# Three fused matmul stages on one core: operand addresses of the wide products, landing times in the planner, and the pace of the second MLP's weight conversions

## Chip, core and metric

One core of a Trainium2 chip runs the whole program. The metric is the device time of one execution in microseconds; the median of three runs is given. The program uses TensorE (products), VectorE and ScalarE (element-wise work), GpSimd (some transfers) and SyncE's queue (most transfers).

## What is computed

A linear attention without softmax, whose output goes through two MLPs, all to float32 accuracy:

```python
kv = np.einsum('bhsd,bhse->bhde', k, v)            # 8 x 8 heads, 576 tokens, 64 wide
out = np.einsum('bhsd,bhde->bhse', q, kv)
x = out / np.sqrt(np.mean(out * out, -1) + 1e-6) * g_norm   # 4608 tokens x 512

h = x @ w_in                                       # 512 -> 2048
x = (s * np.maximum(h, 0) ** 2 + b) @ w_out        # 2048 -> 512
h = x @ w_in2
return (h * np.cos(h)) @ w_out2
```

The MLP weights arrive as float64, the rest as float32, and the weights are turned into float32 pairs on the chip.

## The kernel before

**Products.** A *product* is one MATMUL instruction: 128x128 weights are loaded (LDWEIGHTS) and 256, 384 or 512 columns stream through them from SBUF into a PSUM bank. To keep float32 accuracy every operand is split into a high and a low part of type float32r, and one mathematical product is three instructions: high x high, high x low, low x high. Each product has its own weight load, and the weights of the next product load while the present one streams.

**Stages.** Up to about 360 us: attention, interleaved with the first three blocks of 512 tokens of the first MLP. There `mm_h` (L724 to L726) streams x (512 columns, tiles X in the tile `shared`) through w_in (tiles WI), `act1` makes g (tiles G), and `mm_o` (L781, for the first twelve weight tiles of block 0 L773 in plain float32) streams g through w_out (tiles WO). From there on the work goes in *pairs* (two tiles of 128 hidden columns, 768 tokens): 32 pairs for the rest of the first MLP (about 362 to 880 us), then 48 for the second. `mm_h2` (L932) computes h by a scheme with seven instead of eight half-size block multiplications: seven *chains* of six products of 384 columns, in the order 0, 1, 5, 4, 6, 2, 3. It streams sums and differences of quarter blocks of x (`x_sums`; slots in `shared`, G, `late` and WI) through prepared weight sums that `w_load` brings in from DRAM into the ring WI[0:6]. ScalarE copies the chains' banks out (`snap`, L944), VectorE adds them to h (L948). In the first MLP `act1_pair` (L1002, L1003, L1005, L1007) makes g as high and low parts in WI[6:], and `mm_o1` (L827) streams them through w_out, 512 and 256 columns. In the second MLP `act2` does it, and `mm_o` (L781) has g's parts (in WI[6:] and `raw`) as weights and streams w_out2 (512 columns).

**Conversions.** During the first MLP's pairs the second MLP's 32 weight tiles are converted (`conv2`, `w_conv`): a load of raw bits into the one tile `raw`, ScalarE L382 (the first to need the load) and L392, VectorE L383 to L400, and for w_in2 sums of two tiles (`w_sums`, L454). `split_store` (L436, L437) splits the result into tiles T, which go to DRAM (L444) and come back later as weights. A T tile is free again when its store has landed; `snap` uses the same five T tiles in the first MLP's pairs.

**What sets the order.** Nothing is ordered by hand. Every step is an `op` with an engine, a cost and a due time; `Plan.run` plays them through a model of the engines and queues: at each step it takes the engine that can start first, and on it the op with the earliest due time among those that can start within 0.1 us. A tile slot is given to the op that starts, if the model says that its last reader (for a store, its landing) is done. The order that comes out is the program's order on each engine, and the engines then wait for each other by semaphores. A transfer of the model lands 0.5 us (`LANDS`) after its modelled time on the DMA engines. `sref` makes a tile in a slot; its argument `shift` is an offset in elements from the slot's start, in the tiles WI and RAW alone.

## Time and profile before

| what | value |
|---|---|
| median of 3 runs | 1625.25 us (1623.31 to 1625.88) |
| the profiled execution | 1624.52 us |
| its span, first to last instruction | 1622.7 us |
| TensorE busy | 1610.5 us, 9952 products recorded |
| VectorE, ScalarE busy | 1101.8 us, 872.0 us |
| pairs of the first MLP, undisturbed | 15.64 us each |
| pairs of the second MLP | 15.52 us each |

A float32 product is recorded as two, so 9952 records stand for 8864 instructions; 3504 of them are float32r products of 512 columns, 768 of 256 and 3360 of 384. A product's record starts when it starts to stream and ends when its last column is through, so records overlap: the time of one product in a row of many is the distance between starts, and its record lasts some 0.16 us longer. Idle time of TensorE is therefore seen shortened by that much.

### The profile page before, as it was taken

To read this page: it belongs to the slowest core of one execution; us is meant where nothing else is said; L and a number is where in the kernel's file an instruction comes from. 1 tells how busy PE (TensorE), PEld (TensorE's weight loads), DVE (VectorE), ACT (ScalarE), POOL (GpSimd) and SP (SyncE) were. 2 spreads that over 40 slices of the span, in tenths; PEclk is the share of its full clock that TensorE was granted. 3 is DMA by queue.
4 is the path that set the end of the run, shared out by engine and by line. 5 is a ranking of instruction groups with operands and counts; after the bars stand their busy time and mean duration, and the time that the engine had idled before them with its cause. 6 is when DMAs were issued, how large, how long until landed. Compare 5 with 4: busy or idle time off the path is not lost.

```text
span 1622.7 us, 26185 instructions
## 1 busy us (share of the span) xinstructions
PE 1610.5 (99%) x9952; PEld 1423.7 (88%) x9952; DVE 1101.8 (68%) x1832; ACT 872.0 (54%) x1483; POOL 54.5 (3%) x90
## 2 busy tenths in 40 slices
PE   8999999999999999999999999999999999999998
PEld 7668888789999999989999989989899898998997
DVE  6887776675776777776446667667668668568564
ACT  5865543355565565555435455545546546446543
POOL 0011222100000000000000000000000000000000
PEclk9999999999999999999999999999999999999999
DMA  9746878936778878876656445544444544444531
GB/s 319 224 102 175 217 192 204 249 123 227 246 232 267 274 218 276 261 224 203 223 180 229 160 123 149 169 124 139 167 131 136 172 117 137 164 133 129 156 117 47
DMA packets 198285, 297.44 MB, mean 183 GB/s; under 512 B 81936, under 2 KB 124432, under 8 KB 198160
## 3 DMA queue, kind: packets, MB, share of 16 engines
q1 hardware_dynamic: 191568, 274.20, 54.5%
q0 software_dynamic: 6016, 20.45, 4.6%
q8 instruction: 79, 1.29, 0.3%
q10 hardware_dynamic: 576, 1.11, 0.2%
q14 instruction: 46, 0.38, 0.1%
HBM read 232.79 MB, written 62.91 MB: 182 GB/s over the span
## 4 chain that ended last, share of the span: by engine, by line
PE 94%; DMA 3%; DVE 1%; ACT 1%; issue 0%; POOL 0%; SPq 0%; ACTq 0%; POOLq 0%; DVEq 0%
PE banks L932 35%; PE banks L781 30%; PE banks L827 14%; PE banks L724 3%; PE banks L773 3%; PE banks L725 3%; PE banks L726 3%; PE banks L550 1%; PE banks L644 1%; DMA raw<-in_moe_w_out_dram 1%; PE banks L682 1%; DMA w2i_d<-t 1%; DMA wi<-w1i_d 1%; PE banks L1019 1%; DMA raw<-in_moe_w_in_dram 0%; DMA x_d<-t 0%
## 5 line engine op out<-in xcount | busy, mean ns | idle before, releaser
L932 PE MATMUL banks<-shared,wi 128*128 128x384 f32 x2232 | 441.0, 336 | 0.8 <-ACT t L944 0.7
L932 PEld LDWEIGHTS banks<-shared,wi 128*128 128x128 f32 x2232 | 390.6, 188 | 13.8 <-ACT t L944 2.2
L781 PE MATMUL banks<-wo,wi 128*128 128x512 f32 x1446 | 372.6, 391 | 0.0
L781 PEld LDWEIGHTS banks<-wo,wi 128*128 128x128 f32 x1446 | 269.9, 188 | 49.9
L827 PE MATMUL banks<-wi,wo 128*128 128x512 f32 (+1 forms) x1536 | 288.6, 336 | 0.8 <-DVE wi L1007 0.8
L827 PEld LDWEIGHTS banks<-wi,wo 128*128 128x128 f32 x1536 | 244.1, 188 | 29.7 <-DVE wi L1007 1.3
L944 ACT COPY t<-banks 128x384 f32<-128x384 f32 x235 | 112.3, 479 | 215.2 <-PE banks L932 199.1
L986 ACT ACTIVATE wi<-wi 128x768 f32<-128x768 f32 x96 | 81.3, 847 | 79.6 <-DVE wi L984 79.6
L932 PE MATMUL banks<-late,wi 128*128 128x384 f32 x552 | 111.7, 336 | 0.0
L932 PE MATMUL banks<-g,wi 128*128 128x384 f32 x504 | 110.1, 337 | 1.0 <-ACT t L944 0.8
L781 PE MATMUL banks<-g,wo 128*128 128x512 f32 x432 | 108.3, 394 | 0.0
L978 ACT ACTIVATE wi<-wi 128x768 f32<-128x768 f32 x95 | 79.9, 846 | 46.2 <-DVE wi L948 44.9
L932 PEld LDWEIGHTS banks<-late,wi 128*128 128x128 f32 x552 | 97.2, 188 | 3.3
L948 DVE TENSOR_TENSOR wi<-banks,t 128x384 f32<-128x384 f32 x128 | 71.2, 556 | 40.3 <-PE banks L932 33.9
L781 PEld LDWEIGHTS banks<-g,wo 128*128 128x128 f32 x432 | 79.9, 188 | 17.3
L932 PEld LDWEIGHTS banks<-g,wi 128*128 128x128 f32 x504 | 89.2, 188 | 6.5 <-ACT t L944 2.2
L982 DVE SCALAR_TENSOR_TENSOR wi<-wi,wi 128x768 f32<-128x768 f32 x95 | 90.8, 956 | 1.7
L988 DVE TENSOR_TENSOR wi<-wi,wi 128x768 f32<-128x768 f32 x95 | 90.6, 954 | 1.5
L781 PE MATMUL banks<-wo,raw 128*128 128x512 f32 x282 | 88.3, 393 | 0.0
L980 DVE TENSOR_SCALAR wi<-wi 128x768 f32<-128x768 f32 x96 | 53.7, 559 | 50.2 <-ACT wi L978 48.9
L724 PE MATMUL banks<-shared,wi 128*128 128x512 f32 x192 | 82.4, 429 | 2.5 <-ACT shared L701 1.6
L1003 DVE SCALAR_TENSOR_TENSOR wi<-wi,small,wi 128x768 f32<-128x768 f32 x64 | 64.8, 1016 | 23.5 <-ACT wi L1002 23.3
(155 smaller groups left out, 2090.9 us busy)
## 6 DMA issues: line engine op xcount, KB each, us to landing
wi<-w2i_d SPq DMA_DIRECT2D x144, 512.0 KB, 4.2
wi<-w1i_d SPq DMA_DIRECT2D x96, 512.0 KB, 4.7
late<-x_d SPq DMA_DIRECT2D x36, 384.0 KB, 6.0
w2i_d<-t SPq DMA_DIRECT2D x48, 256.0 KB, 4.5
wi<-w2i_d SPq DMA_DIRECT2D x48, 256.0 KB, 2.7
x_d<-t SPq DMA_DIRECT2D x40, 256.0 KB, 3.0
wi<-in_moe_w_in_dram SPq DMA_DIRECT2D x16, 512.0 KB, 9.2
wo<-in_moe_w_out_dram SPq DMA_DIRECT2D x16, 512.0 KB, 9.6
```

What stands on the lines that cost most here:

```text
L724: nc.tensor.matmul(h.t, wh, hi, start=(c == 0), stop=False)
L781: nc.tensor.matmul(o.t, a, b, start=(first and z == 0), stop=(last and z == 2))
L827: nc.tensor.matmul(dst, x[:, sl], y[:, src], start=(first and z == i == 0), stop=(last and z == 2), skip_group_check=a >= 4)
L932: nc.tensor.matmul(o.t[:, 0:HT], a, b, start=(first and c == z == 0), stop=(c == 1 and z == 2), skip_group_check=not first)
L944: op("ACT", 0.38, by + 1, lambda: nc.scalar.copy(dst(), o.t[:, 0:HT]), p=[s], r=[o])
L948: op("DVE", 0.475, by + 1, lambda: nc.vector.tensor_tensor(out=h[f].t[:, half * HT:(half + 1) * HT], in0=a.t[:, 0:HT], in1=s.t, op=ALU.add ...
L978: op("ACT", act, by, lambda u=u, x=x: nc.scalar.activation(u.t, x.t, AF.Identity, scale=1.0 / TWO_PI, bias=0.25), w=[u], r=[x])
L980: op("DVE", two, by + 1, lambda u=u: nc.vector.tensor_scalar(out=u.t, in0=u.t, scalar1=MAGIC, scalar2=-MAGIC, op0=ALU.add, op1=ALU.add), w ...
L982: op("DVE", one, by + 2, lambda u=u, x=x: nc.vector.scalar_tensor_tensor(out=u.t, in0=x.t, scalar=1.0 / TWO_PI, in1=u.t, op0=ALU.mult, op1 ...
L986: op("ACT", act, by + 4, lambda u=u: nc.scalar.activation(u.t, u.t, AF.Sin, scale=TWO_PI, bias=0.5 * math.pi), w=[u])
L988: op("DVE", one, by + 5, lambda u=u, x=x: nc.vector.tensor_tensor(out=u.t, in0=u.t, in1=x.t, op=ALU.mult), w=[u], r=[x])
L1003: op("DVE", 0.93, by + 2, lambda u=u, x=x: nc.vector.scalar_tensor_tensor(out=u.t, in0=u.t, scalar=s_sb, in1=x.t, op0=ALU.mult, op1=ALU.mu ...
```

## The change

Three edits go together.

**Addresses.** `sref` takes a table from a slot's prefix to an offset, and the tiles that it shifts begin elsewhere. Modulo 128 bytes (all tile distances of a kind are multiples of it, so it is the same for a whole line) the difference between the address from which a product streams and the address of the weights of the next product of its line is, in the two built programs:

| products | streamed, weights | before | after |
|---|---|---|---|
| L724 to L726, 512 columns, 576 | X in `shared`, WI | 64 | 16 |
| L781 in the first MLP, 512 columns, 432 | G, WO | 0 | 16 |
| L827, 512 and 256 columns, 768 each | WI, WO | 64 | 16 |
| L781 in the second MLP, 512 columns, 1728 | WO, WI or RAW | 64 | 16 |
| L932, 384 columns, 3360 | `shared`, G, late or WI, ring WI | 64 | 64 |
| L932 followed by L781 of the second MLP | | 64 | 16 |
| L932 followed by L827 | | 0 | 0 |

The streamed tiles move in the first three rows, the weights in the fourth.

**Landing.** An op has a new field `late`, which the planner adds to the landing of a transfer: 2.0 us for the raw loads of the second MLP's weights, 1.5 us for the stores of split weights.

**Pace.** The 32 conversions of the second MLP are called for over 25 pairs instead of 22.

```diff
-    def op(self, eng, cost, due, fn, w=(), p=(), r=(), keep=(), after=()):
+    def op(self, eng, cost, due, fn, w=(), p=(), r=(), keep=(), after=(), late=0.0):
...
-                end = seen = dma + self.LANDS
+                end = seen = dma + self.LANDS + o.late
...
-    shared = sb.tile([P, 33 * 256], F32R, name="shared")
+    EDGE = (4, 16)
+    shared = sb.tile([P, 33 * 256 + EDGE[1]], F32R, name="shared")
+    WIDE = 1024 + 64
...
-                t, at = shared, plan.parts[s].start * 256
-            elif shift and s in WI + RAW:
-                t, at = sb.tile([P, 1024], dtype, tag=s, name=s), shift
+                t, at = shared, plan.parts[s].start // 2 * 256 + EDGE[plan.parts[s].start % 2]
+            elif shift and s[:2] in shift or s in G:
+                t, at = sb.tile([P, WIDE if s in G else 1024], dtype, tag=s, name=s), shift.get(s[:2], 0)
...
+    OFF = {s: 4 for s in slots("g", 3)}
...
-        plan.parts[s] = range(4 * n, 4 * n + 4)
+        plan.parts[s] = range(8 * n, 8 * n + 8)
...
-        plan.parts[s] = range(3 * n, 3 * n + 3)
+        plan.parts[s] = range(6 * n + 1, 6 * n + 7)
...
-        op("SP", 1.45 if kind == "i" else 1.35, by - 12 if load_by is None else load_by, load, w=[raw], after=after)
+        op("SP", 1.45 if kind == "i" else 1.35, by - 12 if load_by is None else load_by, load, w=[raw], after=after,
+           late=2.0 if ph else 0.0)
...
-            op("SP", n * 0.0013, by, store, p=[ref], r=[part])
+            op("SP", n * 0.0013, by, store, p=[ref], r=[part], late=1.5)
...
-            g = sref(G)
+            g = sref(G, shift=OFF)
...
-            x = x2f[j, k, c] = sref(XF if j else XF0, F32R, (2, HT), 16)
+            x = x2f[j, k, c] = sref(XF if j else XF0, F32R, (2, HT), {"wi": 16})
...
-            u, hi, lo = sref(ACTS, F32, (TB2,)), *(sref(PARTS, F32R, (TB2,)) for z in range(2))
+            u, hi, lo = sref(ACTS, F32, (TB2,)), *(sref(PARTS, F32R, (TB2,), {"wi": 12, "ra": 12}) for z in range(2))
...
-            u, hi, lo = sref(ACTS1, F32, (TB2,), 32), *(sref(ACTS1, F32R, (TB2,), 32) for z in range(2))
+            u, hi, lo = sref(ACTS1, F32, (TB2,), {"wi": 20}), *(sref(ACTS1, F32R, (TB2,), {"wi": 20}) for z in range(2))
...
-                done_convs - EARLY_CONVS) * (NP1 - 10) <= (n - 1) * (4 * NU - EARLY_CONVS):
+                done_convs - EARLY_CONVS) * (NP1 - 7) <= (n - 1) * (4 * NU - EARLY_CONVS):
```

The second and third edit change the order on all engines from about 150 us on; up to there it is the same. Lines of the new kernel are five higher from `mm_h` and `act1` on (L944 is L949, L1003 is L1008). Two places follow, with the tiles' numbers.

ScalarE in pair 22, a raw weight's first step (L382, now L387) among the copies of chains (L944, now L949). Before:

```order
L944 COPY t2_7814<-banks_77 128x384
L382 ACTIVATE c2_7816<-raw_7751 128x512
L944 COPY t0_7824<-banks_77 128x384
L944 COPY t4_7841<-banks_77 128x384
L392 ACTIVATE raw_7751<-raw_7751 128x512
```

Now:

```order
L949 COPY t3_7751<-banks_77 128x384
L387 ACTIVATE c3_7785<-raw_7733 128x512
L949 COPY t1_7793<-banks_77 128x384
L949 COPY t2_7799<-banks_77 128x384
L397 ACTIVATE raw_7733<-raw_7733 128x512
```

The raw step still stands between the copies; over the whole program it stands directly ahead of a copy in 18 of 32 conversions before and in 17 of 32 now.

ScalarE from the end of pair 22 to the first copy of pair 23 (the last row of each), where the next block's x is split (L885, now L890). Before:

```order
L1002 ACTIVATE wi14_7864<-wi13_7846 128x768
L436 CAST t0_7871<-c2_7816 128x512
L944 COPY wi8_7804<-banks_77 128x384
L1002 ACTIVATE wi11_7881<-wi8_7804 128x768
L1005 ACTIVATE wi9_7892<-wi14_7864,small_125 128x768
L1005 ACTIVATE wi13_7903<-wi11_7881,small_125 128x768
L382 ACTIVATE c4_7911<-raw_7866 128x512
L885 CAST shared_76<-late3_7407 128x384
L885 CAST shared_76<-t1_7471 128x384
L885 CAST shared_76<-t3_7489 128x384
L392 ACTIVATE raw_7866<-raw_7866 128x512
L944 COPY t2_7957<-banks_77 128x384
```

Now:

```order
L1007 ACTIVATE wi7_7828<-wi6_7808 128x768
L441 CAST t1_7840<-c3_7785 128x256
L1007 ACTIVATE wi15_7844<-wi14_7727 128x768
L441 CAST t3_7858<-c1_7842 128x512
L890 CAST shared_76<-late3_7341 128x384
L890 CAST shared_76<-t4_7470 128x384
L890 CAST shared_76<-t0_7501 128x384
L890 CAST late4_7887<-late0_7324 128x384
L1010 ACTIVATE wi9_7890<-wi7_7828,small_125 128x768
L1010 ACTIVATE wi12_7902<-wi15_7844,small_125 128x768
L441 CAST t2_7906<-c0_7833 128x512
L949 COPY t3_7910<-banks_77 128x384
```

The two steps that make g's high parts (L1005, now L1010) came before the splits and now come after four of them, followed by a split of w_sums' result (L441).

VectorE at the same place. Before:

```order
L948 TENSOR_TENSOR wi13_7846<-banks_77,t2_7814 128x384
L400 ISA c2_7816<-raw_7751,c2_7816 128x1024
L1003 SCALAR_TENSOR_TENSOR wi14_7864<-wi14_7864,small_125,wi13_7846 128x768
L437 TENSOR_TENSOR t4_7883<-c2_7816,t0_7871 128x512
L1003 SCALAR_TENSOR_TENSOR wi11_7881<-wi11_7881,small_125,wi8_7804 128x768
L1007 SCALAR_TENSOR_TENSOR wi10_7901<-wi14_7864,small_125,wi9_7892 128x768
L1007 SCALAR_TENSOR_TENSOR wi8_7913<-wi11_7881,small_125,wi13_7903 128x768
```

Now:

```order
L459 TENSOR_TENSOR c0_7833<-c3_7785,c4_7557 128x256
L459 TENSOR_TENSOR c1_7842<-c3_7785,c0_7833 128x256
L442 TENSOR_TENSOR t2_7846<-c3_7785,t1_7840 128x256
L459 TENSOR_TENSOR c1_7842<-c4_7557,c1_7842 128x256
L459 TENSOR_TENSOR c0_7833<-c3_7785 128x256
L1008 SCALAR_TENSOR_TENSOR wi7_7828<-wi7_7828,small_125,wi6_7808 128x768
L891 TENSOR_TENSOR shared_76<-late3_7341,shared_76 128x384
L891 TENSOR_TENSOR shared_76<-t4_7470,shared_76 128x384
L891 TENSOR_TENSOR shared_76<-t0_7501,shared_76 128x384
L895 TENSOR_TENSOR t4_7470<-t4_7470,late0_7324 128x384
L895 TENSOR_TENSOR t0_7501<-t0_7501,late2_7334 128x384
L1008 SCALAR_TENSOR_TENSOR wi15_7844<-wi15_7844,small_125,wi14_7727 128x768
```

Both L1003 of the pair stood near the raw step L400; now four w_sums (L459), and x's splits and differences (L891, L895) stand ahead of the first or the second L1008.

## Rows read from the trace of the kernel before

**Rows 1.** The page: busy time, share of the span and instructions of each engine.

```profile
PE 1610.5 (99%) x9952; PEld 1423.7 (88%) x9952; DVE 1101.8 (68%) x1832; ACT 872.0 (54%) x1483; POOL 54.5 (3%) x90
```

**Rows 2.** Stretches: start:end, length, busy us by engine, granted clock, DMA share, GB/s.

```profile
378.00:484.00 106.00, 105.22 (x597) 97.04 (x597) 75.09 (x126) 61.88 (x106) 0.00 (x0) 1.00 0.74 243
484.00:738.00 254.00, 252.20 (x1443) 233.81 (x1442) 184.66 (x310) 148.99 (x256) 0.00 (x0) 1.00 0.78 251
738.00:863.00 125.00, 125.00 (x722) 116.92 (x721) 62.69 (x89) 57.99 (x95) 0.00 (x0) 1.00 0.61 206
888.00:1602.00 714.00, 714.00 (x3591) 645.97 (x3590) 485.60 (x724) 375.69 (x592) 0.00 (x0) 1.00 0.45 140
```

**Rows 3.** L781's products, 329 to 332 and 1120 to 1126 us: duration ns min/median/max.

```profile
L781 PE MATMUL banks<-g,wo x12: 388/389/389, 329.2 to 331.7; 128*128 128x512 f32 x12
...
L781 PE MATMUL banks<-wo,wi x23: 388/392/394, 1120.8 to 1125.9; 128*128 128x512 f32 x23
```

**Rows 4.** Timeline of TensorE, three places: start, us, engine, line, what, count.

```profile
327.15 0.39 PE L724 MATMUL banks<-shared,wi 128*128 128x512 f32 x1
...
329.22 2.88 PE L781 MATMUL banks<-g,wo 128*128 128x512 f32 x12
331.94 0.39 PE L724 MATMUL banks<-shared,wi 128*128 128x512 f32 x1
...
342.72 2.92 PE L781 MATMUL banks<-g,wo 128*128 128x512 f32 x12
...
786.85 0.87 PE L827 MATMUL banks<-wi,wo 128*128 128x256 f32 x6
787.55 2.25 PE L932 MATMUL banks<-shared,wi 128*128 128x384 f32 x12
...
794.18 6.38 PE L827 MATMUL banks<-wi,wo 128*128 128x512 f32 x30
800.41 0.85 PE L932 MATMUL banks<-shared,wi 128*128 128x384 f32 x4
...
1119.79 1.20 PE L932 MATMUL banks<-shared,wi 128*128 128x384 f32 x6
1120.83 6.34 PE L781 MATMUL banks<-wo,wi 128*128 128x512 f32 x27
```

**Rows 5.** L932's products, 780 to 830 and 1000 to 1100 us, as rows 3.

```profile
L932 PE MATMUL banks<-shared,wi x81: 332/336/340, 784.8 to 825.3; 128*128 128x384 f32 x81
...
L932 PE MATMUL banks<-shared,wi x204: 336/336/336, 1003.9 to 1097.9; 128*128 128x384 f32 x102
```

**Rows 6.** Timeline near 510 us; in brackets the idle time and its releaser.

```profile
509.44 0.67 ACT L382 ACTIVATE c<-raw 128x512 f32<-128x512 f32 x1 [4.05 <-DMA raw<-in_moe_w_out_dram]
...
510.70 0.97 PE L932 MATMUL banks<-shared,wi 128*128 128x384 f32 x4 [0.66 <-ACT t L944]
```

**Rows 7.** Groups, 380 to 870 us: busy us, mean ns | idle; one timeline row.

```profile
L1003 DVE SCALAR_TENSOR_TENSOR wi<-wi,small,wi 128x768 f32<-128x768 f32 x62 | 62.8, 1017 | 23.5 <-ACT wi L1002 23.3
...
L944 ACT COPY t<-banks 128x384 f32<-128x384 f32 x123 | 58.7, 478 | 95.1 <-PE banks L932 79.1 <-DMA w2i_d<-t 9.2 <-DVE wi L948 1.8
L1005 ACT ACTIVATE wi<-wi,small 128x768 fp32r<-128x768 f32 x62 | 57.6, 933 | 10.9 <-DVE wi L1003 7.7 <-PE banks L827 2.9
...
L948 DVE TENSOR_TENSOR wi<-banks,t 128x384 f32<-128x384 f32 x61 | 33.9, 555 | 28.3 <-PE banks L932 22.0 <-ACT t L944 3.7 <-PE banks L827 1.9
...
L436 ACT CAST t<-c 128x512 fp32r<-128x512 f32 x40 | 24.3, 617 | 7.5 <-DVE c L400 3.9 <-DMA w2i_d<-t 2.5 <-DVE wi L948 0.6
...
L400 DVE CUSTOM_DVE_ANT_0 c<-raw,c 128x1024 uint16<-128x1024 uint16 x32 | 22.0, 688 | 7.1 <-ACT raw L392 6.5
...
L382 ACT ACTIVATE c<-raw 128x512 f32<-128x512 f32 x31 | 20.7, 667 | 39.3 <-DMA raw<-in_moe_w_out_dram 26.8 <-DMA raw<-in_moe_w_in_dram 12.4
...
L454 DVE TENSOR_TENSOR c<-c,c 128x256 f32<-128x256 f32 x24 | 10.1, 420 | 0.3
...
724.10 1.02 DVE L886 TENSOR_TENSOR shared<-t,shared 128x384 fp32r<-128x384 f32 x2
```

More of the change, by code (lines that the diff above doesn't have):

```diff
@@ L83, in __init__ @@
         self.parts = {}
-    def op(self, eng, cost, due, fn, w=(), p=(), r=(), keep=(), after=()):
+    def op(self, eng, cost, due, fn, w=(), p=(), r=(), keep=(), after=(), late=0.0):
         o = Op()
-        o.eng, o.cost, o.due, o.fn, o.refs = eng, cost, due, fn, list(dict.fromkeys([*w, *p, *r, *keep]))
+        o.eng, o.cost, o.due, o.fn, o.late = eng, cost, due, fn, late
+        o.refs = list(dict.fromkeys([*w, *p, *r, *keep]))
         deps = set(after)
@@ L254, in pool_of, with sref @@
         return sb
-    shared = sb.tile([P, 33 * 256], F32R, name="shared")
-    def sref(slots, dtype=F32, shape=(512,), shift=0):
+    EDGE = (4, 16)
+    shared = sb.tile([P, 33 * 256 + EDGE[1]], F32R, name="shared")
+    WIDE = 1024 + 64
+    def sref(slots, dtype=F32, shape=(512,), shift=None):
         def make(s):
@@ L300, in fused_kernel @@
     for s in [*WO, *G, *T, *C]:
-        sb.tile([P, 512 if s in T + C else 1024], F32, tag=s, name=s)
+        sb.tile([P, 512 if s in T + C else WIDE if s in G else 1024], F32, tag=s, name=s)
     sb.tile([P, 48], F32, tag="between", name="between")
@@ L322, in fused_kernel @@
         kv_f[divmod(n, KC)] = sref([KV_F[n]], F32, (D,))
-    small = cpool.tile([P, 20], F32, name="small")
+    small = cpool.tile([P, 8], F32, name="small")
     g_sb, s_sb, b_sb, spare = (small[:, i:i + 1] for i in range(4))
@@ L747, in act1 @@
         if i in WHOLE:
-            g = sref(G)
+            g = sref(G, shift=OFF)
             if i in ON_ACT:
@@ L755, in act1 @@
             return g
-        g = sref(G, F32R, (2, TB))
+        g = sref(G, F32R, (2, TB), OFF)
         op("ACT", 0.62, by - 1, lambda: nc.scalar.activation(g.t[:, 0], t.t, AF.Identity, bias=b_sb),
@@ L920, in mm_h2 @@
         t0 = pair_due(n)
-        h = [sref(ACTS, F32, (TB2,)) if n >= NP1 else sref(ACTS1, F32, (TB2,), 32) for f in range(2)]
+        h = [sref(ACTS, F32, (TB2,)) if n >= NP1 else sref(ACTS1, F32, (TB2,), {"wi": 20}) for f in range(2)]
         order = (0, 1, 5, 4, 6, 2, 3)
```

## The prediction

> **What bounds the kernel now.** I read the page first. TensorE is busy 99% of the span, VectorE and ScalarE 68% and 54% [rows 1], and TensorE's granted clock is 1.00, its upper level of 2.4 GHz, in every stretch [rows 2]. So the time is the sum of the products (one product is one MATMUL instruction), and there are two ways to shorten it: less time from the start of one product to the start of the next, or less waiting. The view by stretches sizes the second: between 738 and 863 us and from 888 us on, TensorE is busy for the whole stretch; between 378 and 738 us it lacks 0.78 + 1.80 us [rows 2]. A wait shows shortened, since the 0.16 us by which a product's record outlasts its successor's start (389 ns against 227 ns [rows 3, 4]) counts as busy; with some seven waits about 3.7 us are lost there. The rest is the rate.
>
> The rate is read from the timeline. Twelve 512-column products of the first MLP's second matmul run from 329.22 to 331.94 us: 2.72 / 12 = 226.7 ns each. The nine before them (L724 to L726) take (329.22 - 327.15) / 9 = 230.0 ns. In the second MLP 27 of them take (6.34 - 0.39) / 26 = 228.8 ns, and at L827, between 794.18 and 800.41 us, 24 of 512 and 6 of 256 columns take 6.23 us; six of 256 columns take 0.70 us (786.85 to 787.55), which leaves 230.3 ns for one of 512 [rows 4]. At 2.4 GHz 512 columns stream in 213.3 ns, so every product has 13 to 17 ns on top. Three things tell me that part of this hangs on where the operands lie. The extra is steady, not noise: the settled products by g last 388 to 389 ns, those by wo 388 to 394 [rows 3]. Between these groups the residue of (address of the streamed operand minus address of the next weights, modulo 128 bytes) differs: 0 for g, 64 for the other three. And the 384-column products, residue 64 among themselves, last exactly 336 ns in a stretch of the second MLP, but up to 340 where the first MLP's L827, with residue 0, comes next [rows 5].
>
> **The change, part by part.** *Residue 16 for all products of 512 and 256 columns.* No row has residue 16, so the price is bounded from rows. Nearest to 16 is 0, and the settled row of residue 0 is 226.7 ns; that is the value I take. L781 of the second MLP: 1728 x (228.8 - 226.7) = 3.6 us. L827: 768 x (230.3 - 226.7) = 2.8 us. L724 to L726: 576 x (230.0 - 226.7) = 1.9 us. L781 of the first MLP is at 0 now; a run of twelve takes 2.72 us when settled, and the most it could give is 432 x 3.3 ns = 1.4 us; I take 0.5. The 768 products of 256 columns: 0, since no row shows them at another residue; bounds 768 x 4 ns = 3 us either way. Where a 384-column product is followed by L781 (some 185 places) the residue goes from 64 to 16: 0 to 185 x 4 ns = 0.7 us lost [rows 5], I take 0.4. The 384-column products keep 64: nothing. Sum: -8.4 us. Bounds of this term: below, the 256-column products, whose extra is 116.7 - 106.7 = 10.0 ns, would make a 512-column product 223.3 ns, 3504 x (229.2 - 223.3) = -21 us (229.2 is the mean of the four rates above, by count); above, what residue 0 does to a 384-column product, +4 ns, is 3504 x 4 = +14 us. The other end of the shift costs nothing I can find: the shifted tiles are written and read by VectorE and ScalarE alone, no DMA touches them, and both engines have slack [rows 1].
>
> A rule of the Trainium skill speaks against this part. SBUF — State Buffer, section "Who interferes with whom", gives TensorE two independent read ports, one for the streamed operand and one for weights, and has TensorE wait for nobody. By that rule an address could not matter and the term would be 0. The trace does not agree: 226.7 against 228.8 to 230.3 ns for the same 512 columns.
>
> *Later landings in the planner's model, conversions over 25 pairs.* These move instructions and add none: still 32 conversions, each of one raw load, seven ACT and DVE steps and stores. What they can give back is the waits of the stretch 484 to 738 us. Two are typical: ScalarE stands 4.05 us at L382 until a raw weight has landed, the copy L944 behind it empties a PSUM bank late, and TensorE loses 0.66 us [rows 6]. ScalarE waits 39.3 us for raw weights in all and 9.2 us at L944 for stores [rows 7], yet TensorE loses only the 1.80 us of rows 2 plus six tails of 0.16, 2.8 us. The rows of order say that the pattern survives: L382 stands directly ahead of a copy L944 in 18 of 32 conversions before and in 17 of 32 after. So I take half, -1.4 us (bounds -2.8 and 0). Spreading moves the last conversions to pair 26, near 780 us, where TensorE waits for nothing at a DMA share of 0.61; I cost that at nothing. If that cover were gone, it would be one or two waits like that of rows 6, under 2 us.
>
> What they can take is at the pairs where the next block's x is split. In pair 22 the new order puts a conversion's w_sums (L459), then three splits and two sums of x (L891, L895) ahead of the pair's second L1008; before, both L1003 came first. From the total L953 that ends the pair's sixth chain of products to the first copy of pair 23 stand, at the durations of rows 7: L953 0.56, L405 0.69, four L459 at 0.42, L442 (of the same size) 0.42, L1008 1.02, five L891 and L895 at 0.55, L1008 1.02, then on ScalarE L1010 0.93, L441 0.62 and L949 0.48, 10.2 us in all. Two steps of 384 columns in a row (L886) take 1.02 us where one (L948) lasts 0.555 [rows 7], so each of the 13 steps on VectorE starts 0.08 us before its predecessor's end: 9.1 us. TensorE's work in that time is the last chain (6 x 173.3 = 1.04 us), nine products of 512 (2.1), twelve of 384 (2.1) and eighteen of 256 columns (2.1), 7.3 us, and the next chain needs the bank which that copy empties. So TensorE waits about 1.8 us. I take +1.8 for this place, and +1.0 (bounds 0 and 3.8) for the same collision at the two other x splits of this stage, near pairs 7 and 15, whose order I read less closely. What is queued behind: every ScalarE copy of pair 23, so VectorE's totals wait too. Net of the planner's part: +1.4 us, bounds -2.8 and +5.6.
>
> Sum: -8.4 + 1.4 = -7.0 us on the profiled execution's 1624.52 us. It lies 0.7 us below the median of the runs, 1625.25, so the forecast for the median is 1618.3, said as 1618.
>
> **The rivals.** (A) *A lower floor.* Residue 16 is neither 0 nor 64, and 0 and 64 may both be bad: then a product may fall to the 223.3 ns of the 256-column bound or further, -21 + 1.4: 1606. For it: the 256-column products show that the extra can be less than 13.3 ns. Against it: residue 0 at 512 columns and residue 64 at 384 (1.04 us for six, 173.3 ns, where 160 would stream [rows 4]) stop at the same 13.3 ns, as if that were a floor. TensorE: Matmul & The Clock Gate, section "Back-to-back issue gap", has N / 2.4 + 2.5 ns, 215.8 for 512 columns; the sum by it would be 3504 x 13.4 = 47 us, 1580, and no row comes near that rate.
>
> (B) *The address decides nothing*, and the 226.7 ns belongs to something else in those runs (g is rewritten for each run, wo and wi are not). Then only the planner's part is left: 1625.25 + 1.4 = 1627, from 1622 to 1631. For it: a run of twelve by g at 342.72 us takes (2.92 - 0.39) / 11 = 230 ns, with the same addresses [rows 4]. Against it: the 384-column products, where clock, width and streamed tiles are the same and only the weights that follow differ [rows 5].
>
> (C) *Slower:* residue 16 acts on 512 columns as 0 does on 384, streamed operand and next weights meeting again and again. Place: every one of the 3504 products; price +4 ns each [rows 5], +14 + 1.4: 1641. It decides as soon as a 512-column product takes more than today's mean of 229.2 ns. For it: 16 is near to 0, and 0 is what costs the 384-column products. Against it: 0 is the better of the two for 512.
>
> (D) *The order eats the gain:* collisions like pair 23's at all three x splits and none of the raw waits gone, +5.6 - 8.4: 1622.5.
>
> **How the numbers follow.** Forecast 0.50 (its own range 1613 to 1624), A 0.16, B 0.17, C 0.10, D 0.07. A measurement of this kernel can tell about 0.2% from no change, 1622.0 to 1628.5. Faster: 0.43 of the forecast, all of A and 0.01 of B, 0.60. Same: the 0.07 left of the forecast, 0.05 of D, 0.12 of B, 0.24. Slower: C, 0.04 of B and 0.02 of D, 0.16. The range leaves out the lower half of A, C and the upper edge of B, 0.2 in all: 1604 to 1630.
>
> **What would show it.** In the timeline of the new kernel 27 products of L786 should take 6.28 us from first start to last end where 6.34 stand now, and a pair of the second MLP 15.44 us where 15.52 is 42 x 173.3 + 36 x 228.8 ns. If that run stays at 6.34, B holds; at 6.2 or less, A; above 6.36, C. The 384-column records should stay at 336 ns. For the planner's part: a wait of about 1.8 us for ScalarE's L949 at the start of pair 23, near 720 us, and fewer waits for L949 behind L387. I am wrong in the sum if the stretch from 484 to 738 us loses more than 9 us or nothing at all.

## The result, and the profile after

The changed kernel takes 1635.67 us (median of 4, 1634.67 to 1637.59) against 1625.57 us (1623.31 to 1626.21): a ratio of 1.0070, 95% interval 1.0058 to 1.0081. It is 10 us slower, where 7 us less were forecast. The profiled execution spans 1632.9 us where it spanned 1622.7 us. The page after:

```profile
span 1632.9 us, 26159 instructions
...
PE 1615.8 (99%) x9952; PEld 1426.7 (87%) x9952; DVE 1102.7 (68%) x1832; ACT 871.5 (53%) x1483; POOL 54.5 (3%) x90
```

TensorE is still busy 99% of the span, but its busy time itself is 5.3 us more [rows 1]. Busy time contains slow products and the last 0.16 us of each wait, so it does not part the two terms. Stretches answering to [rows 2], with the same columns:

```profile
378.00:484.00 106.00, 105.00 (x598) 97.05 (x599) 72.94 (x125) 60.82 (x103) 0.00 (x0) 1.00 0.71 234
484.00:738.00 254.00, 249.32 (x1411) 230.64 (x1410) 172.74 (x284) 139.95 (x240) 0.00 (x0) 0.99 0.73 235
738.00:863.00 125.00, 123.62 (x710) 115.19 (x709) 70.98 (x110) 60.30 (x101) 0.00 (x0) 1.00 0.69 229
```

TensorE lacks 1.00 + 4.68 + 1.38 = 7.06 us here, against 0.78 + 1.80 + 0 = 2.58 us before. That is 4.5 us more idle time. The rate, in the timeline of TensorE (start, us, line, what, count), at a place of the first MLP and one of the second:

```profile
340.04 0.39 PE L729 MATMUL banks<-shared,wi 128*128 128x512 f32 x1
...
342.82 2.24 PE L786 MATMUL banks<-g,wo 128*128 128x512 f32 x9
344.90 1.20 PE L937 MATMUL banks<-shared,wi 128*128 128x384 f32 x6
...
1131.44 6.33 PE L786 MATMUL banks<-wo,wi 128*128 128x512 f32 x27
1137.61 0.69 PE L937 MATMUL banks<-late,wi 128*128 128x384 f32 x3
```

Twelve products of L729 to L731 take 342.82 - 340.04 = 2.78 us, 231.7 ns each, where they took 230.0 [rows 4]. Nine by g take 2.08 us, 231.1 ns each, where settled ones took 226.7. The 27 of the second MLP take 6.17 us from first start to the next line's start, 228.5 ns each, where they took 228.8. So in these rows residue 16 costs 2 to 4 ns in the first MLP and gives 0.3 in the second. Over all long runs of L781 and L786 in the second MLP the starts show a fixed pattern. Before, 229.2, 231.7 and 225.8 ns repeat, 228.9 on the mean. Now three of about 229.1 and one of 225.8 repeat, 228.3 on the mean. The 231.7 are gone, but the 225.8 come every fourth time instead of every third; why was not found.

From the distances between starts in both traces, by line, the 10.2 us of span come out as follows.

| part | us |
|---|---|
| L729 to L731: 576 x 2.2 ns | +1.3 |
| L786, first MLP: 432 x 2.6 ns | +1.1 |
| L832, 512 columns: 768 x 1.5 ns | +1.2 |
| L832, 256 columns: 768 x 0.7 ns | +0.5 |
| L786, second MLP: 1543 (those followed by their like) x -0.7 ns | -1.1 |
| L937, second MLP: 2016 x 0.2 ns | +0.4 |
| TensorE's waits over 50 ns and products at half clock, 8.3 to 16.0 us | +7.7 |
| not assigned | -0.9 |

The row of L937 is made by the first product behind each run of L786, 175 to 176 ns where 173.3 stood.

The largest wait is at the place that the prediction names, the start of pair 23. Timeline after (idle time and its releaser in brackets):

```profile
723.18 0.56 DVE L953 TENSOR_TENSOR wi<-banks,t 128x384 f32<-128x384 f32 x1 [0.84 <-PE banks L937]
...
724.23 0.48 ACT L949 COPY wi<-banks 128x384 f32<-128x384 f32 x1 [2.50 <-PE banks L937]
...
724.38 0.89 DVE L459 TENSOR_TENSOR c<-c,c 128x256 f32<-128x256 f32 x2
...
725.78 0.43 DVE L442 TENSOR_TENSOR t<-c,t 128x256 fp32r<-128x256 f32 x1 [0.51 <-ACT t L441]
...
726.12 0.42 DVE L459 TENSOR_TENSOR c<-c,c 128x256 f32<-128x256 f32 x1
726.45 0.42 DVE L459 TENSOR_TENSOR c<-c 128x256 f32<-128x256 f32 x1
...
728.20 2.30 PE L832 MATMUL banks<-wi,wo 128*128 128x256 f32 x18
...
730.06 1.01 DVE L1008 SCALAR_TENSOR_TENSOR wi<-wi,small,wi 128x768 f32<-128x768 f32 x1
...
731.11 0.93 ACT L1010 ACTIVATE wi<-wi,small 128x768 fp32r<-128x768 f32 x1 [1.35 <-DVE wi L1008]
...
732.07 0.62 ACT L441 CAST t<-c 128x512 fp32r<-128x512 f32 x1
...
732.81 0.48 ACT L949 COPY t<-banks 128x384 f32<-128x384 f32 x1
...
733.35 0.80 PE L937 MATMUL banks<-shared,wi 128*128 128x384 f32 x3 [2.85 <-ACT t L949]
```

From the start of the total L953 at 723.18 us to the end of the copy L949 at 733.29 us pass 10.1 us. Between the copy of 724.23 us and that of 732.81 us ScalarE runs no copy of a chain. TensorE's records end at 730.50 us and the next starts at 733.35, 2.85 us later; against the usual distance between starts it loses 3.0 us. A second place is new: the block's x goes to DRAM from the same T tiles.

```profile
764.86 4.32 SPq L848 DMA_DIRECT2D x_d<-t  x3
766.69 0.48 ACT L949 COPY t<-banks 128x384 f32<-128x384 f32 x1 [1.97 <-DMA x_d<-t]
...
767.22 0.80 PE L937 MATMUL banks<-shared,wi 128*128 128x384 f32 x3 [1.38 <-ACT t L949]
```

L949 stands 1.97 us until a store of x (L848) has landed and freed its T tile, and TensorE loses 1.4 us.

### The profile page after: what moved, and what is told of

It reads as the page before. It is cut to its first block, busy times and chain, and to the rows that moved or that the text cites. A ratio compares the mean times of both kernels' runs of the same rounds, so it can differ in the third digit from the quotient of the medians.

```text
span 1632.9 us, 26159 instructions
## 1 busy us (share of the span) xinstructions
PE 1615.8 (99%) x9952; PEld 1426.7 (87%) x9952; DVE 1102.7 (68%) x1832; ACT 871.5 (53%) x1483; POOL 54.5 (3%) x90
## 4 chain that ended last, share of the span: by engine, by line
PE 96%; DMA 2%; ACT 1%; DVE 1%; issue 0%; POOL 0%; SPq 0%; POOLq 0%; ACTq 0%; DVEq 0%
PE banks L937 35%; PE banks L786 30%; PE banks L832 15%; PE banks L729 3%; PE banks L730 3%; PE banks L731 3%; PE banks L778 3%; PE banks L555 1%; PE banks L649 1%; DMA w2i_d<-t 1%; PE banks L687 1%; PE banks L1024 1%; DMA x_d<-t 0%; PE banks L563 0%; DMA raw<-in_moe_w_in_dram 0%; PE banks L610 0%
## 5 line engine op out<-in xcount | busy, mean ns | idle before, releaser
L937 PE MATMUL banks<-shared,wi 128*128 128x384 f32 x2232 | 456.2, 337 | 5.3 <-ACT t L949 4.6
L937 PEld LDWEIGHTS banks<-shared,wi 128*128 128x128 f32 x2232 | 391.8, 188 | 17.8 <-ACT t L949 6.5
L786 PE MATMUL banks<-wo,wi 128*128 128x512 f32 x1446 | 371.9, 390 | 0.0
L786 PEld LDWEIGHTS banks<-wo,wi 128*128 128x128 f32 x1446 | 269.7, 188 | 49.3
L832 PE MATMUL banks<-wi,wo 128*128 128x512 f32 (+1 forms) x1536 | 289.3, 337 | 0.9 <-DVE wi L1012 0.9
L832 PEld LDWEIGHTS banks<-wi,wo 128*128 128x128 f32 x1536 | 244.7, 188 | 30.6 <-DVE wi L1012 1.4
L949 ACT COPY t<-banks 128x384 f32<-128x384 f32 x235 | 112.2, 478 | 224.1 <-PE banks L937 202.2
L937 PE MATMUL banks<-g,wi 128*128 128x384 f32 x528 | 119.5, 337 | 0.8 <-DVE wi L953 0.8
L937 PE MATMUL banks<-late,wi 128*128 128x384 f32 x528 | 113.6, 338 | 0.0
L786 PE MATMUL banks<-g,wo 128*128 128x512 f32 x432 | 108.7, 397 | 0.0
L953 DVE TENSOR_TENSOR wi<-banks,t 128x384 f32<-128x384 f32 x128 | 71.2, 557 | 53.4 <-PE banks L937 45.9
L937 PEld LDWEIGHTS banks<-late,wi 128*128 128x128 f32 x528 | 94.7, 189 | 5.0
L937 PEld LDWEIGHTS banks<-g,wi 128*128 128x128 f32 x528 | 94.3, 188 | 5.2 <-DVE wi L953 1.2
L786 PEld LDWEIGHTS banks<-g,wo 128*128 128x128 f32 x432 | 80.1, 188 | 18.2
L786 PE MATMUL banks<-wo,raw 128*128 128x512 f32 x282 | 87.7, 390 | 0.0
L729 PE MATMUL banks<-shared,wi 128*128 128x512 f32 x192 | 82.7, 431 | 1.9 <-ACT shared L706 1.6
L1008 DVE SCALAR_TENSOR_TENSOR wi<-wi,small,wi 128x768 f32<-128x768 f32 x64 | 64.7, 1016 | 25.8 <-ACT wi L1007 25.3
```

The source lines that it names most:

```text
L729: nc.tensor.matmul(h.t, wh, hi, start=(c == 0), stop=False)
L786: nc.tensor.matmul(o.t, a, b, start=(first and z == 0), stop=(last and z == 2))
L832: nc.tensor.matmul(dst, x[:, sl], y[:, src], start=(first and z == i == 0), stop=(last and z == 2), skip_group_check=a >= 4)
L937: nc.tensor.matmul(o.t[:, 0:HT], a, b, start=(first and c == z == 0), stop=(c == 1 and z == 2), skip_group_check=not first)
L949: op("ACT", 0.38, by + 1, lambda: nc.scalar.copy(dst(), o.t[:, 0:HT]), p=[s], r=[o])
L953: op("DVE", 0.475, by + 1, lambda: nc.vector.tensor_tensor(out=h[f].t[:, half * HT:(half + 1) * HT], in0=a.t[:, 0:HT], in1=s.t, op=ALU.add ...
```

## The experiments

Three theories stood after the first look. **1**: both parts cost, the addresses some 3 us and the order some 7. **2**: residue 16 gives the forecast 8 us and the order takes more than that back. **3**: the addresses are neutral. Every comparison is with runs of the kernel before on the same chip, 21 to 27 of them. Two more kernels, e7_residues and e11_parts_apart, ran once each for their traces (1629.86 and 1630.23 us) and are not compared by time.

| run | median, us | ratio to before | 95% interval |
|---|---|---|---|
| e1_addresses | 1626.57 | 1.0014 | 1.0005 to 1.0023 |
| e2_planner | 1631.11 | 1.0045 | 1.0032 to 1.0057 |
| e3_landings | 1631.87 | 1.0045 | 1.0033 to 1.0057 |
| e4_pace | 1623.65 | 0.9997 | 0.9989 to 1.0006 |
| e5_raw_landing | 1625.62 | 1.0007 | 0.9998 to 1.0016 |
| e6_store_landing | 1629.11 | 1.0030 | 1.0019 to 1.0042 |
| e8_no_call_at_split | 1628.16 | 1.0023 | 1.0014 to 1.0032 |
| e9_low_priority | 1622.90 | 0.9992 | 0.9983 to 1.0001 |
| e10_pace28 | 1624.38 | 1.0000 | 0.9992 to 1.0009 |
| e12_store_half | 1622.75 | 0.9993 | 0.9984 to 1.0002 |
| e13_best_parts | 1625.44 | 1.0007 | 0.9998 to 1.0016 |
| e14_after_low_priority | 1626.62 | 1.0015 | 1.0006 to 1.0025 |

### The parts of the change apart

**Addresses alone.** Against the kernel after:

```diff
-           late=2.0 if ph else 0.0)
+           late=0.0)
...
-            op("SP", n * 0.0013, by, store, p=[ref], r=[part], late=1.5)
+            op("SP", n * 0.0013, by, store, p=[ref], r=[part])
...
-                done_convs - EARLY_CONVS) * (NP1 - 7) <= (n - 1) * (4 * NU - EARLY_CONVS):
+                done_convs - EARLY_CONVS) * (NP1 - 10) <= (n - 1) * (4 * NU - EARLY_CONVS):
```

> The new addresses alone (landings and pace of before, so every engine runs the order of before). The two traces have the 27 products of the second MLP at 6.34 us before and 6.33 us after, those of L724 to L726 at 228.6 to 230.2 ns before and 231.2 to 232.0 ns after, so theory 1, that residue 16 is worth nothing and costs a little in the first MLP, expects 1625.6 + 3 = 1629 us (1627 to 1631), with the waits of before. Theory 2, that residue 16 does give the forecast 8 us and the new order hides it, expects 1617 us. Theory 3, that the addresses are neutral and the whole loss is the order's, expects 1625.6 us within 1 us.

Measured: +0.14%, 2.3 us (0.8 to 3.7). Theory 2 falls. Theory 1 comes nearest, though 1626.57 us lies 0.4 us below its range. Theory 3 falls by the rates rather than by the time, since the interval's lower end is within its 1 us. The profiled span grew by 1.8 us: the rates as in the table above, less somewhat over 1 us of waits that happened to be shorter.

**Planner alone.** The three other edits on the kernel before.

> Later landings and 25 pairs alone, at the addresses of before; every engine runs the order of after. Theory 1 expects the waits of after (3.0 us near 730, 1.5 us near 765, the slow products behind the first) and 1625.6 + 7 = 1632.5 us (1631 to 1634). Theory 2 expects 1625.6 + 18 = 1643 us. Theory 3 expects 1635.7 us.

Measured: +0.45%, 7.3 us by the ratio, as theory 1 has it. With e1 that makes 9.6 of the 10.1 us.

**Landings alone, pace alone.** The `late` terms with `NP1 - 10`, and `NP1 - 7` without them, both at the addresses of before.

> Later landings alone, 22 pairs and addresses of before. If the waits of after come from the pace, which puts conversions into pairs 22 to 25 where x is split and the block before is stored, this has no wait of over 1 us after 700 us and takes 1624 to 1627 us. If they come from the changed landings, it takes 1631 us or more.

> 25 pairs alone, landings and addresses of before. If the pace is what costs, the waits of after near 730 and 765 us are here too and it takes 1630 to 1633 us; if it needs both edits, or the landings alone, 1624 to 1627 us.

The pace costs nothing (-0.03%); the landings cost all of it (+0.45%). TensorE's busy time from 378 to 738 us, pace alone:

```profile
378.00:738.00 360.00, 358.78 (x2053) 333.34 (x2052) 255.81 (x417) 209.15 (x353) 0.00 (x0) 1.00 0.74 240
```

and landings alone:

```profile
378.00:738.00 360.00, 352.67 (x2014) 325.89 (x2013) 251.47 (x417) 205.93 (x353) 0.00 (x0) 1.00 0.75 241
```

The pace leaves TensorE 1.22 us of idle time in that stretch, the landings 7.33 us; before it was 0.78 + 1.80 [rows 2]. Yet the landings did what they were made for. The group of the raw step in the landings kernel, 380 to 870 us (busy, mean | idle before it):

```profile
L382 ACT ACTIVATE c<-raw 128x512 f32<-128x512 f32 x31 | 20.6, 664 | 14.1 <-DMA raw<-in_moe_w_in_dram 8.5 <-DMA raw<-in_moe_w_out_dram 5.6
```

ScalarE's wait for raw weights fell from 39.3 us [rows 7] to 14.1 us, while TensorE lost 4.8 us more. With the pace alone that wait stays at 37.3 us, and TensorE loses less than before, 1.22 us. So TensorE's loss does not follow ScalarE's wait. (In the kernel after, with both edits, the wait is 27.7 us.)

**Which landing.** Kernel before with `late=1.5` at the raw loads alone (the change has 2.0), and with `late=1.5` at the stores alone.

> Kernel before with later landings in the model for the raw loads alone (1.5 us; with 2.0 us alone the planner finds no order). Both landings together cost 0.45%, 7 us. If it is the raw loads, whose one tile makes each conversion wait for the one before, so that the last conversion starts 18 us later (749 against 731 us) and meets more of the splits of x, this takes 1629 to 1632 us. If it is the stores, 1623 to 1627 us. If both share it, 1627 to 1629 us.

> Kernel before with later landings in the model for the stores of split weights alone (1.5 us). If the raw loads are what costs, this takes 1623 to 1627 us, and its last conversion starts near 731 us; if it is the stores, which hold the five T tiles longer in the model and so move the copies of chains, 1629 to 1632 us; if both share it, 1627 to 1629 us.

Raw loads +0.07%, not clear of nothing; stores +0.30%. TensorE from 378 to 738 us and the raw step from 380 to 870 us, raw loads alone:

```profile
378.00:738.00 360.00, 356.46 (x2033) 330.19 (x2032) 254.63 (x422) 208.76 (x357) 0.00 (x0) 1.00 0.77 245
```

```profile
L382 ACT ACTIVATE c<-raw 128x512 f32<-128x512 f32 x31 | 20.7, 668 | 13.7 <-DMA raw<-in_moe_w_in_dram 8.7 <-DMA raw<-in_moe_w_out_dram 4.9
```

and stores alone:

```profile
378.00:738.00 360.00, 353.11 (x2008) 326.34 (x2007) 258.30 (x429) 208.04 (x354) 0.00 (x0) 1.00 0.76 245
```

```profile
L382 ACT ACTIVATE c<-raw 128x512 f32<-128x512 f32 x31 | 20.7, 667 | 38.3 <-DMA raw<-in_moe_w_out_dram 20.2 <-DMA raw<-in_moe_w_in_dram 17.9
```

The two halves of the landings run's result come from different edits. Later raw loads take ScalarE's wait from 39.3 to 13.7 us, and TensorE's idle time does not fall: it goes from 2.58 to 3.54 us. Later stores leave that wait at 38.3 us, and TensorE is idle for 6.89 us; what they shorten is ScalarE's wait for stores at L944, from 9.2 [rows 7] to 1.7 us.

So it is mostly the stores that cost, and the explanation offered for the raw loads falls: in e6 the last conversion starts at 729 us, no later than before (731), and it is e6 that is slow. How a place of e6 loses time, and the same place before:

```profile
444.77 0.66 ACT L382 ACTIVATE c<-raw 128x512 f32<-128x512 f32 x1 [3.31 <-DMA raw<-in_moe_w_out_dram]
445.46 0.43 DVE L383 TENSOR_SCALAR c<-c 128x512 f32<-128x512 f32 x1 [5.03 <-ACT c L382]
445.81 1.01 DVE L1007 SCALAR_TENSOR_TENSOR wi<-wi,small,wi 128x768 fp32r<-128x768 f32 x1
...
446.88 2.50 PE L827 MATMUL banks<-wi,wo 128*128 128x512 f32 x5 [2.30 <-DVE wi L1007]
```

```profile
444.29 1.02 DVE L1007 SCALAR_TENSOR_TENSOR wi<-wi,small,wi 128x768 fp32r<-128x768 f32 x1 [3.40 <-PE banks L827]
444.85 0.67 ACT L382 ACTIVATE c<-raw 128x512 f32<-128x512 f32 x1 [2.92 <-DMA raw<-in_moe_w_out_dram]
...
445.36 1.44 PE L827 MATMUL banks<-wi,wo 128*128 128x512 f32 x5 [0.77 <-DVE wi L1007]
```

In e6 VectorE's order has the raw step's successor L383 ahead of the pair's L1007. VectorE stands idle for 5.03 us until L382 is done, which itself waits for a load. L1007, needed by TensorE, waits behind it, and TensorE stands 2.30 us. Before, L1007 came ahead of L383, started 1.5 us earlier, and TensorE stood 0.77 us. VectorE is not short of time there; one early conversion step in front of a pair step is enough.

### Where the conversions stand

**No conversion called for at the splits of x.** On the kernel after:

```diff
-        while n and n < NP1 and done_convs < 4 * NU and (
+        while n and n < NP1 and n % 8 != 6 and done_convs < 4 * NU and (
```

> Kernel after, but no conversion is called for in pairs 6, 14 and 22, so the raw steps and splits of weights stand clear of most splits of x, where the waits of 3.0 and 0.7 us are. If the meeting of the two is what costs, TensorE loses nothing over 1 us between 690 and 740 us and keeps its full clock there, and it takes 1629 to 1631 us (1635.7 less 5 to 6). If the loss lies in the later landings as such, wherever the conversions stand, 1634 to 1637 us.

Measured: +0.23% over before, 7.5 us under the kernel after, with the landings, the pace and the addresses all left in. Between 690 and 740 us TensorE has no wait of over 50 ns. At the split before it, near 603 us, waits of 0.83 and 0.95 us remain, so the calls left out do not clear every split. The stretch of 378 to 738 us:

```profile
378.00:738.00 360.00, 356.72 (x2034) 330.72 (x2034) 243.03 (x400) 201.03 (x344) 0.00 (x0) 1.00 0.71 230
```

3.28 us idle, where the kernel after has 5.68. More came back than the 5 to 6 us expected; the wait of 1.4 us at 765 us is gone too.

**Lower priority.** The three planner edits at the addresses of before, and the due times of conversions two pairs later, on which the planner's choice among startable steps rests:

```diff
-            conv2(pair_due(n + 1), [done[n - 1]])
+            conv2(pair_due(n + 3), [done[n - 1]])
```

> Later landings and 25 pairs at the addresses of before (1631.1 us), but every conversion is called for with due times two pairs later, so that a pair's own step goes first wherever both could start. If the loss comes from conversions that the later landings make overdue, so that they go ahead of the pair's own steps, the waits of 2.1 and 3.2 us near 692 and 728 us are gone and it takes 1623 to 1627 us. If the later landings cost by holding the T tiles and the one raw tile longer, whatever goes first, 1629 to 1632 us.

Measured: -0.08%, by the ratios 0.53% or 8.6 us under e2_planner. TensorE, 378 to 738 us, and the raw step, 380 to 870 us:

```profile
378.00:738.00 360.00, 359.15 (x2061) 334.09 (x2060) 244.10 (x399) 202.27 (x345) 0.00 (x0) 1.00 0.71 229
```

```profile
L382 ACT ACTIVATE c<-raw 128x512 f32<-128x512 f32 x31 | 20.7, 668 | 13.8 <-DMA raw<-in_moe_w_out_dram 7.7 <-DMA raw<-in_moe_w_in_dram 6.0
```

0.85 us of TensorE's time is lost, the least of the runs so far, and ScalarE waits 13.8 us for raw weights. The first case of the expectation holds: with the T tiles and `raw` held as long as in e2 in the model, the cost is gone. The last conversion starts at 804 us (784 in e2), so standing late is not what costs. At pair 23:

```profile
719.19 1.95 DVE L1003 SCALAR_TENSOR_TENSOR wi<-wi,small,wi 128x768 f32<-128x768 f32 x2 [1.15 <-ACT wi L1002]
...
721.54 0.47 ACT L944 COPY t<-banks 128x384 f32<-128x384 f32 x1
...
722.32 0.94 ACT L1005 ACTIVATE wi<-wi,small 128x768 fp32r<-128x768 f32 x1
...
724.27 0.47 ACT L944 COPY t<-banks 128x384 f32<-128x384 f32 x1
```

The two L1003 stand together, before the sums for w_in2, and two copies L944 stand between splits of x (721.54, 724.27). The splits themselves are the same. That a conversion step goes ahead because the later landing made it overdue is the reading that foretold this run; the due times that the planner compared at each wait were not read out. The later due times also move the conversions to other places, so the two are not told apart here. Lower priority without the later landings was not run by itself; the next kernel comes nearest to it.

**A wider pace, half a landing.** Kernel before with `NP1 - 4`, `pair_due(n + 2)` and g's parts of the second MLP 48 bytes on; then the same with `late=0.5` at the stores.

> Kernel before without later landings; conversions over 28 pairs and due one pair later, and in the second MLP alone g's parts begin 48 bytes on (residue 16, 0.7 ns less per product of 1543 seen). The pace alone gave 1623.65 against 1624.85 us; with 1.1 us of the address and one wait of 0.6 us less, 1621 to 1623 us if pace and priority are what counts; 1624 to 1626 us if the pace is indifferent.

> As the 28-pair kernel with one difference: stores of split weights land 0.5 us later in the model (the change: 1.5 us, and 2.0 us for raw loads, which stay as before here). If any later landing of the stores costs in proportion (1.5 us cost 4.6 us), this is 1 to 2 us slower than the 28-pair kernel. If the cost comes only where conversions meet pair steps, it is within 1 us of it or faster.

1.0000 and 0.9993, each with an interval of 0.09% to either side. The 28 pairs and the one pair of lower priority gave nothing: the products of the second MLP are the 0.6 ns shorter that the address gives, but from 378 to 738 us TensorE idles for 3.45 us where it idled for 2.58. Later stores by 0.5 us cost nothing on top, but the conversions here are due one pair later, which in e9 took the cost of 1.5 us away; half a landing at the old due times was not run. Neither kernel beats the kernel before clear of noise.

### What an address is worth

**All eight residues.** The kernel before with

```diff
-            u, hi, lo = sref(ACTS, F32, (TB2,)), *(sref(PARTS, F32R, (TB2,)) for z in range(2))
+            u, hi, lo = sref(ACTS, F32, (TB2,)), *(sref(PARTS, F32R, (TB2,), 4 * (n % 8)) for z in range(2))
...
-            u, hi, lo = sref(ACTS1, F32, (TB2,), 32), *(sref(ACTS1, F32R, (TB2,), 32) for z in range(2))
+            u, hi, lo = sref(ACTS1, F32, (TB2,), 32), *(sref(ACTS1, F32R, (TB2,), 32 + 4 * (n % 8)) for z in range(2))
```

> Kernel before, with the order of before, but g's parts of pair n begin 16 x (n mod 8) bytes further on, in both MLPs: the residue takes all eight multiples of 16 in turn. If the address decides nothing (theory 1), 512 columns take 228 to 230 ns at every residue. If 16 is merely a wrong choice (theory 2), some residue is at 226 ns or less and another at 232 or more. L827 streams the shifted tile (residue 64 + 16 x (n mod 8) modulo 128), the second MLP's L781 has it as weights (64 - 16 x (n mod 8)): if what counts is the streamed operand's own address and not the difference, the two differ in which residues are dear.

Timeline of TensorE in two neighbouring pairs, residue 16 (935.78 us) and 112 (966.83 us):

```profile
935.78 6.33 PE L781 MATMUL banks<-wo,wi 128*128 128x512 f32 x27
941.94 0.69 PE L932 MATMUL banks<-g,wi 128*128 128x384 f32 x3
...
966.83 6.46 PE L781 MATMUL banks<-wo,wi 128*128 128x512 f32 x27
973.13 0.69 PE L932 MATMUL banks<-g,wi 128*128 128x384 f32 x3
```

27 products take 6.16 us at one address and 6.30 us at the other. Every pair of a residue repeats its value within 1 ns. Residue 96 has runs of 18 there, 233.0 ns a product. The others, from the starts, with the product of L932 ahead of the run and the first of the run:

| residue, second MLP | 27 products, us | ns each | first product, ns | L932 ahead, ns |
|---|---|---|---|---|
| 0 | 6.156 | 228.0 | 241 | 177.5 |
| 16 | 6.164 | 228.3 | 229 | 173.3 |
| 64 | 6.180 | 228.9 | 229 | 173.4 |
| 48 | 6.267 | 232.1 | 234 | 177.7 |
| 80 | 6.291 | 233.0 | 229 | 176 |
| 32 | 6.298 | 233.3 | 231 | 172 |
| 112 | 6.300 | 233.3 | 236 | 177.3 |

A residue always meets the same of the eight pairs of a block in this run. The kernel before is the control: there all eight take 228.9 ns a product, so it is not the pair. So the address counts, and theory 1 as worded in this expectation falls: 5 ns lie between the best and the worst. Theory 2 holds by half, since none is at 226 ns. And 64, where the kernel stood, is within 0.9 ns of the best. For L827 the means are 229.9 (64), 230.7 (112), 231.0 (80), 231.9 (48), 232.1 (16), 232.6 (0), 233.4 (96) and 234.1 ns (32): another order, with 64 the best of all and 16 2.2 ns dearer. A difference modulo 128 alone is therefore not what decides. What decides besides it was not found.

**High and low part apart.** The kernel before with g's two parts at residues of their own.

> Kernel before, with the order of before; the high and the low part of g begin at offsets of their own: in the second MLP residues 0, 8, 16, 64 for each, in the first 64, 112, 80, 48, all 16 pairs of them in turn. If the residue of one product to the next weights alone decides, the time by the next weights' residue repeats the 228.5 (16), 228.9 (0) and 229.2 ns (64) of the sweep whatever the other part has, and 8 lies between 0 and 16. If it takes more than that, some pair of residues is at 227 ns or less, which over 1728 products would be worth 3 us, or the same residue differs by over 2 ns with the other part's.

It takes more than one residue, the second case of the expectation: products whose next weights are at 64 take 227.6 ns where their own weights are at 16, and 231.3 where those are at 8. In runs of 27, from the starts, a product takes 227.5 ns (high 0, low 16), 228.0 (both 0), 228.5 (both 16) and 228.9 ns (both 64, as before); any part at 8 makes it 231 to 235. Over all 36 products of a pair, the short groups with them, the order is another: 228.4 (both 16), 228.9 (both 64), 229.0 (high 0, low 16) and 229.1 ns (both 0).

**The best of these.** The lower-priority kernel with the high part at 0 and the low part at 16 in the second MLP.

> The kernel with lowered priority (later landings, 25 pairs, due two pairs later; 1622.9 us, 0.9992 of before), and in the second MLP alone the high part of g at residue 0 and the low part at 16, the pair that took the least in the run with parts apart: 227.6 against 229.0 ns a product. If what that run showed in three pairs each holds for all 48, 1728 x 1.4 = 2.4 us less, 1620.5 us (0.9977). If those 227.6 ns belonged to the pairs and not to the residues, 1622 to 1624 us.

Measured: 0.15% more than e9 by the ratios, where 0.15% less was expected. Timeline of TensorE in one pair:

```profile
1111.39 0.63 PE L781 MATMUL banks<-wo,raw 128*128 128x512 f32 x2
1111.86 0.40 PE L781 MATMUL banks<-wo,wi 128*128 128x512 f32 x1
1112.09 1.21 PE L932 MATMUL banks<-shared,wi 128*128 128x384 f32 x6
...
1118.73 6.30 PE L781 MATMUL banks<-wo,wi 128*128 128x512 f32 x27
1124.87 1.20 PE L932 MATMUL banks<-late,wi 128*128 128x384 f32 x6
```

The long run takes 6.14 us, 0.04 less than before, and inside it settled products take 226.7 ns. But the first product after L932 takes 241 ns, so a group of three takes 0.70 us (1111.39 to 1112.09), 233 ns each, where it took 0.687 before; a pair has three such groups. That alone uses the gain up, as the 36-product means of the run with parts apart already had it (229.0 against 228.9 ns). The loss is in L932: the product ahead of a run takes 177.4 instead of 173.3 ns and the first two behind it 175 to 179 ns, 1.0 ns on the mean of 2016 products or 2.0 us in all. Switching costs more than settling gives.

### Do the two terms add

The kernel after with `pair_due(n + 3)` for the conversions.

> Kernel after with one change: conversions due two pairs later. If order and addresses simply add, it is the low-priority kernel's 1622.9 us plus the 2.3 us of the addresses, 1625 us (1624 to 1626.5), 10 us under after. If the new addresses also cost through the waits (1635.7 is 1.8 us more than 1625.6 + 2.3 + 6.0), 1627 us or more.

Measured 1626.62 us, 1.0015 of before: 9 us of the 10 come back by one number. It is 0.23% over e9, against 0.14% for the addresses alone, each within 0.09%. So the terms add within what was measured.

## Why the prediction was wrong, point by point

**The bound.** That the time is the sum of the products plus waits held: 3.4 us of rate and 7.7 us of waits and their slow products make 11.1 us, 0.9 more than the span's 10.2.

**Residue 16 (-8.4 us forecast, +2.3 measured).** The larger failing step, 10.7 of the 17 us by which the sum was off, is "Nearest to 16 is 0, and the settled row of residue 0 is 226.7 ns; that is the value I take". Three things were wrong with it. Nearness in bytes means nothing: 8 lies between 0 and 16 and is worse than both. A settled run was taken for all places: e13 has the 226.7 ns inside its long runs and still loses, since the first product after L932 takes 241 ns and L932's own products get longer; the run by g at 342.72 us, 230 ns at the same addresses [rows 4], could have told that. And one residue was given to all lines, while L827 prefers 64. The bounds of the term, -21 to +14, did hold the outcome. The 0.4 us set down for L932 next to L781 was right in size, but it falls on the products behind the run and not on those ahead.

**Rival B (the address decides nothing, 1627).** Its time for this term was nearest, and by the sign that the prediction set for it, a run of L786 that stays at 6.34 us, it would hold: 6.33 were measured. Its reason is false: e7 has 5 ns between addresses. **Rival C** ended on the right side. The mean over the 3504 products did rise, from 229.2 to 229.9 ns, but by the first MLP alone and not at every place. That is 2.5 us and not 14; its 1641 us is near by luck, since the planner's part supplied the rest.

**Raw waits (-1.4 us forecast).** Later raw loads alone took away 25.6 of ScalarE's 39.3 us (e5), and TensorE gained nothing by it. In e9, with as short a wait and the path's steps first, TensorE's idle time did fall, from 2.58 to 0.85 us; but in e4 it fell to 1.22 us with the wait nearly whole. Half the loss of a stretch was credited to a wait because it stood there; which step then stands first was not asked.

**Pair 23 (+1.8 us forecast, 3.0 measured, and 1.6 more).** The mechanism was right, place and order too. The chain of steps took 10.1 us; the sum had 10.2 and, less 1.0 us of credit for overlap, 9.1. The overlap is there where one VectorE step follows another (L459 starts at 726.45 us, 0.09 us before the one of 726.12 us ends). What the sum left out eats it up: VectorE stands 0.51 us at L442 until ScalarE's L441 is done, and the last three steps, on ScalarE, take 2.2 us instead of 2.03. TensorE's work was 7.2 us (723.18 to 733.35 less the 3.0 us lost), forecast 7.3. What the prediction left out: eleven products behind the wait ran at half clock.

**Pairs 7 and 15 (+1.0, bounds 0 to 3.8).** TensorE waits 1.0 us between 462 and 477 us and 1.1 us between 603 and 608 us, at places with no such wait before, while a wait of 0.8 us that stood at 445 us is gone. In the bounds.

**Spread to pair 26 at no cost.** One wait of 1.5 us at 765 us, by a store of x holding a T tile: within "one or two waits under 2 us", and should have been in the sum.

**The planner's sum (+1.4, bounds to +5.6).** +7.3. This is the second step that failed, 5.9 of the 17 us. The upper bound failed for want of the half clock, of pairs 21 and 26, and because it looked at x splits alone: it priced collisions of conversions with splits, while e6 shows a conversion step ahead of a pair step costing 1.5 us with no split of x near. **Rival D** was this mechanism, but set against a gain of 8.4 us that was not there. The range, 1604 to 1630, leaned on one estimate of one term.

## What to carry to other kernels

An idle engine that is off the critical path is no reason for an edit: 25 us of ScalarE's waiting for loads were removed and TensorE gained nothing; 7 us of its waiting for stores were removed and TensorE lost 4 us, until the side work was made to yield to the path's own steps. Where an order is planned, give side work due times that let the path's step go first, and look at the order at the few places where two kinds of side work meet. A rate read from a settled run is worth its number only in runs as long; price the first product after each switch as well.

## What the runs showed of the hardware

**The clock after a wait.** Granted clock (before the DMA share) behind the 2.85 us wait and behind the 1.38 us one of the kernel after:

```profile
734.50:737.00 2.50, 2.50 (x9) 2.50 (x9) 2.26 (x5) 1.21 (x3) 0.00 (x0) 0.50 0.42 143
767.20:769.20 2.00, 1.98 (x11) 1.98 (x12) 1.75 (x3) 1.02 (x2) 0.00 (x0) 1.00 0.69 272
```

0.50 is the level of 1.2 GHz. Between 734.20 and 736.76 us products of 384 columns start 320 ns apart. The Trainium skill, TensorE: Matmul & The Clock Gate, section "Back-to-back issue gap", has N / 1.2 for that level, 320 ns: the trace agrees. At the upper level the same section of the Trainium skill has N / 2.4 + 2.5 for products by themselves, 162.5 ns, where 173.3 are measured: no agreement here. The eleven slow products cost 1.6 us on top of the wait. In other runs the granted clock is 0.50 behind waits of 2.30 us (e6, 446.80 to 449.00 us) and 3.09 us (e2, 732.60 to 735.00 us), and 1.00 behind one of 1.96 us (e2, 694.20 to 697.00 us).

**Addresses.** 27 products of 512 columns take 6.156 to 6.300 us by the place of their weights in SBUF alone, same data, same order. The Trainium skill, SBUF — State Buffer, section "Who interferes with whom", has independent ports for the two operands and TensorE waiting for nobody. By that the place of the weights should not count; in this run it does, by 0.14 us in 6.2.
